# A forgetting-attention and gated-FFN kernel: weight loads tied to the vector engine's progress, and a shallower load queue in its scheduler

## The chip, the cores and the metric

The kernel runs on one core of a Trainium2 chip. The core has a matrix engine (TensorE, PE in the profile), a vector engine (VectorE, DVE), an engine for activation functions (ScalarE, ACT), a general-purpose engine (GpSimd, POOL) and a sync engine (SyncE, SP). Each runs its own instruction stream in program order and waits on semaphores for the others. Loads and stores are issued by SP, ACT or POOL and carried out by 16 DMA engines that all of them share. On-chip tiles live in SBUF; PE writes its results into PSUM.

The metric is the device time of the core in microseconds (us), the median of several runs. The profile is of one execution, and its times count from the start of that execution.

## The reference

Eight batches, each with 8 heads, 576 positions and head size 64, go through causal attention with a decay per position, and then through a gated feed-forward layer with a convolution over positions.

```python
# attention: q, k, v are (8, 8, 576, 64), f is (8, 8, 576)
scores = scale * np.matmul(q, k.transpose(0, 1, 3, 2))
cum    = np.cumsum(np.log(np.clip(f, 0.0001, 1.0)), axis=-1)
scores = np.where(causal, -1e9, scores + cum[..., :, None] - cum[..., None, :])
attn   = softmax(scores)                    # written out in the reference
x      = (attn @ v) as (8, 576, 512)
# feed-forward: w_in (512, 1024), conv_w (3, 1024), w_out (1024, 512)
h    = np.maximum(x @ w_in, 0.0)
conv = sum(conv_w[k] * shifted(h, k) for k in range(3))
out  = (h * sigmoid(conv)) @ w_out
```

## The kernel before

The work is cut into half batches of four heads (called `hb`, 16 of them). Each half batch needs its q and k, loaded with a transpose, its v, and a few extra rows of decay sums in the q and k tiles. Four tiles each for q and k (`RING = 4`) let loads run ahead. A pair of heads inside a half batch is numbered `i`.

SP issues the loads of q, k and v. POOL issues the decay rows and the two weight matrices, which are converted from float32 to float16 on their way:

```python
def rows_of(hb):                      # decay rows of a half batch, issued by POOL
    nc.gpsimd.dma_start(tq[0:1, 0:HS], kd[...])
    nc.gpsimd.dma_start(<two rows of tk>, kd[...])

def load_w_out(j):                    # one of four pieces, 256 KB each on chip
    nc.gpsimd.dma_start(w_out_f16[:, 2 * j:2 * j + 2, :], moe_w_out[256 * j:256 * (j + 1), :]...)
```

DVE prepares what has landed. `clamp` rewrites the q or the k tile of a half batch in place, `cast_v` converts v to float16 in three instructions, and `norm` divides an attention output by its row sums:

```python
def clamp(hb, side, h0, nh): nc.vector.tensor_scalar(t, t, lim..., op0=ALU.mult, op1=ALU.add)
def cast_v(hb, p, eng):      eng.tensor_scalar(va[...], vf[...], 1.0, 0.0, ...)
def norm(i):                 nc.vector.reciprocal(rc, O[...]); nc.vector.tensor_tensor(xn, O, rc, ...)
```

PE computes scores, applies them to v (`pv`, into the single PSUM buffer `O`), transposes the normalized result for some batches (`xpose_pe`; the others are transposed by DMA, issued by SP, in `xpose`), and runs the two matrix products of the feed-forward layer, `moe1` with `w_in_f16` and `moe2` with `w_out_f16`.

The order of the instructions is not written by hand. The Python code describes each piece of work as a task with the engine and the time that it is thought to take, the tasks that it comes after, and a key (low keys go first):

```python
def task(engines, after, key, fn, take=None, give=None, lag=0.2, dma=0.0, also=None, behind=None): ...

    if hb in (2, 3):                                  # in the loop over half batches
        for x, j in zip(landed, (2 * hb - 4, 2 * hb - 3)):   # landed: the loads of q and k
            t_wout.append(task({"POOL": 0.8}, [x], 2 * hb - 1.0, lambda j=j: load_w_out(j), lag=2.0, dma=1.7))
    ...
    for p in range(2):
        t_cast[hb, p] = task({"DVE": 0.75 if p == 0 else 0.42}, [t_half or t_v[b]] + ..., 
                             lambda hb=hb, p=p: cast_v(hb, p, nc.vector), lag=0.2)
        if hb == 1 and p:
            t_win = task({"POOL": 1.0}, [t_cast[1, 1]], -0.5, lambda: nc.gpsimd.dma_start(w_in_f16, ...),
                         lag=2.0, dma=6.5)
```

A small list scheduler, `play()`, goes through these tasks when the kernel is built and writes down, engine by engine, the order in which they are emitted. It holds a load on SP back while more than `QUEUED` microseconds of transfers stand ahead of it by its own count:

```python
AHEAD, QUEUED = 10.0, 6.0
...
if dma and e == "SP" and dma_free > clock + QUEUED:
    kept.append((key, k))
    heapq.heappush(heap, (dma_free - QUEUED, -1, None))
    continue
```

What `play()` settles is an order only. On the chip an instruction waits for what its data need: that a tile was written before it is read, and that it is no longer in use before it is overwritten. A task that comes after another in the list, but shares no data with it, waits for nothing on the chip. The loads of the weights are such tasks: nothing has written or read `w_in_f16` or `w_out_f16` before them.

Of the kernel before, what the change touches and what calls it, by code (L numbers as in the profile page):

```python
# [18 lines left out]
def kernel(  # L19
# [11 lines left out]
    nc = tc.nc  # L31
# [37 lines left out]
    w_in_f16 = cpool.tile([128, NCC, D_FF], FP16)  # L69
    w_out_f16 = cpool.tile([128, NFF, D_MODEL], FP16)  # L70
# [62 lines left out]
    def rows_of(hb):  # L133

        tq, tk = stq_t[hb % RING], stk_t[hb % RING]
        c = slice(hb * HH, (hb + 1) * HH)
        nc.gpsimd.dma_start(tq[0:1, 0:HS], kd[0:1, c, :].rearrange("j h s -> j (h s)"))
        row = HS + 64
        nc.gpsimd.dma_start(bass.AP(tensor=tk.tensor, offset=int(tk.offset) + 2 * row,  # L139
                                    ap=[[2 * row, 2], [1, HS]]),  # L140
                            kd[:, c, :].rearrange("j h s -> j (h s)"))

    def load_w_out(j):

        nc.gpsimd.dma_start(w_out_f16[:, 2 * j:2 * j + 2, :],
                            moe_w_out[256 * j:256 * (j + 1), :].rearrange("(ffc p) dm -> p ffc dm", p=128))
# [10 lines left out]
    def cast_v(hb, p, eng):  # L157
        vf, va = vf_t[hb // 2 % 2][:, HH * (hb % 2):HH * (hb % 2 + 1)], va_t[hb % 3]
        if p == 0:
            eng.tensor_scalar(va[:, 0:2, 0:4, 0:64], vf[:, 0:2, 0:4, :], 1.0, 0.0, op0=ALU.mult, op1=ALU.add)  # L160
            eng.tensor_scalar(va[0:SL, :, 4, 0:64], vf[0:SL, :, 4, :], 1.0, 0.0, op0=ALU.mult, op1=ALU.add)
        else:
            eng.tensor_scalar(va[:, 2:4, 0:4, 0:64], vf[:, 2:4, 0:4, :], 1.0, 0.0, op0=ALU.mult, op1=ALU.add)
# [141 lines left out]
    def off_scores(i, s):  # L305
        hb, h = where(i, s)
        sc = sc_of[i, s] = sc_pool.tile([128, 1024], FP32, name="sc")
        for m in (0, 3, 1, 2):
            w = S - 128 * (m + 1)
            scores(sc[:, OFF[m]:OFF[m] + w], hb, h * S + 128 * m, h * S + 128 * (m + 1), w)  # L310
# [5 lines left out]
    def diag_scores(i):  # L316
        sc = sc_of[i, 2] = sc_pool.tile([128, 1024], FP32, name="sc")
        for s in range(2):
            hb, h = where(i, s)
            nc.tensor.matmul(sc[:, 512 * s:512 * (s + 1)], identb, trib, start=True, stop=False,  # L320
                             skip_group_check=True)
            for m in range(4):
                o, c = h * S + 128 * m, 512 * s + 128 * m
                scores(sc[:, c:c + 128], hb, o, o, 128, False, m == 3)
# [57 lines left out]
    def xpose_pe(b, tb):  # L382

        g, j = grp_of[b]
        if tb == 0 and j == 0:
            xt_of[g] = xt_pool.tile([128, NCC, GROUPS[g][1] * S], FP16, name="xt",
                                    padded_shape=[128, NCC, 2 * S])
        n = 128 if tb < NKB - 1 else SL
        ps = mm_of["x", b, tb] = mm_pool.tile([128, 512], FP32, name="mm")
        p16 = ps.bitcast(FP16)  # L390
        for cc in range(NCC):
            nc.tensor.transpose(p16[:, 128 * cc:128 * cc + n],
                                xn_of[b][0:n, tb, 128 * cc:128 * (cc + 1)], ident16[0:n, 0:n])
# [11 lines left out]
    def tiles_of(g):  # L405
        nb = GROUPS[g][1]
        nt = 3 if nb == 2 else 2
        return nt, nb * S // nt

    def moe1(g, ff, t):  # L410
        nt, w = tiles_of(g)
        xt = xt_of[g]
        ps = mm_of[g, ff, t] = mm_pool.tile([128, 512], FP32, name="mm")
        for cc in range(NCC):
            nc.tensor.matmul(ps[:, 0:w], w_in_f16[:, cc, 128 * ff:128 * (ff + 1)],  # L415
                             xt[:, cc, w * t:w * (t + 1)], start=(cc == 0), stop=(cc == NCC - 1))
# [21 lines left out]
    def conv(g, ff, part):  # L438
        nb, ht = GROUPS[g][1], ht_of[g, ff]
        hl, hc, hr = (ht[:, 0:nb, HT_0 + o:HT_0 + o + S] for o in (-1, 0, 1))  # L440
        if part == 0:
            u_of[g, ff] = u_pool.tile([128, nb, S], FP32, name="u", padded_shape=[128, 2, S])
        u = u_of[g, ff]
        if part == 0:
            nc.vector.scalar_tensor_tensor(u, hl, cwt[:, ff, 0:1], hc, op0=ALU.mult, op1=ALU.add)  # L445
        else:
            nc.vector.scalar_tensor_tensor(u, hr, cwt[:, ff, 1:2], u, op0=ALU.mult, op1=ALU.add)  # L447
# [71 lines left out]
    def task(engines, after, key, fn, take=None, give=None, lag=0.2, dma=0.0, also=None, behind=None):  # L519

        tasks.append((engines, key, fn, [r for r in (take, also) if r], give or [], lag, dma))
        after = [a for a in after if a is not None]
        left.append(len(after) + (behind is not None))
        due.append([])
        next_of.append([])
        if behind is not None:
            next_of[behind].append(len(tasks) - 1)
        for a in after:
            due[a].append(len(tasks) - 1)
        return len(tasks) - 1  # L530
# [10 lines left out]
    t_gate, t_cast, t_xt0, t_wout = {}, {}, {}, []  # L541
# [5 lines left out]
    for hb in range(NHB):  # L547
# [3 lines left out]
        even, landed = [], []  # L551
        for s in range(2):
            if hb == 1:
                x = task({"ACT": 0.01}, [], -9, lambda: None, lag=(0.3, 3.8)[s])
# [17 lines left out]
            last = t_v[b] = task({"SP": 3.5}, [t_cast[2 * b - j, p] for j in (4, 3) for p in range(2)] if b >= 2 else [],  # L572
                                 key + 1.2, lambda b=b: load_v(b), lag=2.3, dma=6.0, behind=last)
        if hb in (2, 3):
            for x, j in zip(landed, (2 * hb - 4, 2 * hb - 3)):
                t_wout.append(task({"POOL": 0.8}, [x], 2 * hb - 1.0, lambda j=j: load_w_out(j), lag=2.0, dma=1.7))
        if hb:
            t_rows[hb] = even + [task({"POOL": 1.1}, [landed[0], even[1]], 2 * hb - 3.0 if hb > 1 else -1.0,
# [3 lines left out]
        for p in range(2):  # L582
            t_cast[hb, p] = task({"DVE": 0.75 if p == 0 else 0.42},
                                 [t_half or t_v[b]] + ([t_pv[2 * hb - 5, 1]] if hb >= 3 else []), 2 * hb - 2.1 + 0.5 * p,
                                 lambda hb=hb, p=p: cast_v(hb, p, nc.vector), lag=0.2)
            if hb == 1 and p:
                t_win = task({"POOL": 1.0}, [t_cast[1, 1]], -0.5, lambda: nc.gpsimd.dma_start(
                    w_in_f16, moe_w_in.rearrange("(cc p) ff -> p cc ff", p=128)), lag=2.0, dma=6.5)

        for p in range(2):  # L590
# [3 lines left out]
            if p == 0:  # L594
                x = t_second = task({"ACT": 0.01}, [], -9, lambda: None, lag=3.7) if i == 0 else None
# [5 lines left out]
            x = task({"PE": 0.9}, t_rows[hb], i + 0.1, lambda i=i: diag_scores(i), take="sc")  # L601
            t_qk[hb, p] = [t_tail, x]
            mask = task({"ACT": 1.02}, [x], i + 0.1, lambda i=i: diag_exp(i), take="pm", give=[("sc", x)])
            for s in range(2):
                x = task({"PE": 0.46}, t_rows[hb], i + 0.2 + 0.4 * s, lambda i=i, s=s: off_scores(i, s),
                         take="sc")
# [10 lines left out]
        if hb % 2:  # L617
            norms = [t_norm[i - j] for j in range(PPB)]
            if b in (0, 1, 2, B - 1):
                t_xt[b] = []  # L620
                for tb in range(NKB):
                    x = task({"PE": 0.27}, norms, i + 0.3 + 0.1 * tb, lambda b=b, tb=tb: xpose_pe(b, tb),
                             take="mm", also="xt" if tb == 0 and grp_of[b][1] == 0 else None, behind=x if tb else None)
# [14 lines left out]
    for g, (b0, nb) in enumerate(GROUPS):  # L638
        nt, w = tiles_of(g)
        n = nb * S  # L640
        t_m1, t_tanh = [], []
        for ff in range(NFF):
            key = start[g] + (start[g + 1] - start[g]) * ff / NFF
            relus = []
            for t in range(nt):
                x = task({"PE": 4 * w / 2400.0}, [x for j in range(nb) for x in t_xt[b0 + j]] + [t_win],
                         key + 0.05 * t,
                         lambda g=g, ff=ff, t=t: moe1(g, ff, t), take="mm", also="ht" if t == 0 else None,
                         behind=t_m1[-1] if t else None)
# [5 lines left out]
            x = task({"DVE": 0.23 + n / 1020.0}, [y], key + 0.14, lambda g=g, ff=ff: conv(g, ff, 1))  # L655
            x = task({"ACT": 0.19 + n / 1200.0 + (1.3 if (g, ff) == (LAST, 0) else 0.0)},
                     [x] + (t_tanh[0:1] or t_exp), key - 0.5, lambda g=g, ff=ff: tanh(g, ff),
                     give=[("u", y)], take="hg" if ff == 0 and g % 2 == 0 else None)
# [9 lines left out]
        x = None  # L668
        if g == LAST:
            banks = [task({"PE": 0.01}, t_xt[b0], start[g] + 0.01 * j, lambda p=p, r=r: last_bank(p, r), take=r)  # L670
                     for j, (p, r) in enumerate(((sc_pool, "sc"), (sc_pool, "sc"), (o_pool, "O")))]
            for ff in range(NFF):
                x = task({"PE": 1.1}, [t_gate[g, ff]] + t_wout + banks + [x] * (ff > 0), start[g], lambda ff=ff: moe2_last(ff))
        for c in chunks:
            key = start[g + 1] + (start[g + 2] - start[g + 1]) * (c - chunks[0]) / len(chunks) + 1.0
            if g == LAST:
                x = t_m2[0] if t_m2 else x
            else:
                x = task({"PE": 1.73}, done + t_wout, key, lambda g=g, c=c: moe2(g, c), take="mm")
            t_m2.append(x)  # L680
            x = task({"DVE": 0.62, "ACT": 0.57}, [x] + ([y] if c % 2 else []), key - 1.0,
                     lambda e, g=g, c=c: evac(g, c, e), give=[("mm", x)] if g < LAST else [], take="ob" if c % 2 == 0 else None)
# [4 lines left out]
        if g % 2:  # L687
            task({"SP": 0.01}, t_m2, key, lambda: None, give=[("hg", t_hg)])

    AHEAD, QUEUED = 10.0, 6.0  # L690

    def play():
        busy = {"PE": 11.5, "ACT": 12.0, "DVE": 12.0, "POOL": 14.0, "SP": 19.0}
# [112 lines left out]
```

## Time and profile before

| what | value |
|---|---|
| time, median of 3 runs | 296.53 us (295.26 to 297.28) |
| span of the profiled execution | 293.7 us |
| PE busy | 248.1 us, 84% of the span |
| DVE busy | 220.5 us, 75% |
| ACT busy | 208.3 us, 71% |
| POOL busy | 35.1 us, 12% |
| transfers | 46.64 MB, mean 159 GB/s |

Busy time is a mean over the whole span. The stages differ: by the table of stretches PE was busy for 18.84 of the 20 us from 160 to 180, but for 5.69 of the 10 us from 20 to 30. So a stretch has to be looked at by itself. The chain of work that ended last gives the waits that set the end; an idle time anywhere else costs nothing. In the lines of a timeline, the first two numbers are the start and the duration in microseconds, L and a number is the line of the kernel, and the bracket at the end holds the idle time before the instruction and what ended it. The granted clock (PEclk) is the share of PE's full clock that it was given.

### The profile page before, as it was taken

To read this page: it belongs to the slowest core of one execution; us is meant where nothing else is said; L and a number is where in the kernel's file an instruction comes from. 1 tells how busy PE (TensorE), PEld (TensorE's weight loads), DVE (VectorE), ACT (ScalarE), POOL (GpSimd) and SP (SyncE) were. 2 spreads that over 40 slices of the span, in tenths; PEclk is the share of its full clock that TensorE was granted. 3 is DMA by queue.
4 is the path that set the end of the run, shared out by engine and by line. 5 is a ranking of instruction groups with operands and counts; after the bars stand their busy time and mean duration, and the time that the engine had idled before them with its cause. 6 is when DMAs were issued, how large, how long until landed. Compare 5 with 4: busy or idle time off the path is not lost.

```text
span 293.7 us, 6359 instructions
## 1 busy us (share of the span) xinstructions
PE 248.1 (84%) x2522; PEld 166.8 (57%) x2522; DVE 220.5 (75%) x389; ACT 208.3 (71%) x345; POOL 35.1 (12%) x85
## 2 busy tenths in 40 slices
PE   3784579858899989999799989993999999769980
PEld 1353457635666766766576766662777765434530
DVE  5942335987789989898778999956788887785661
ACT  4265237749678998797887796984689996774651
POOL 4570020202022022022010001210000000000000
PEclk9979558969799999999999999998899999999996
DMA  7999999999999998899799799997114201020114
GB/s 147 226 174 186 217 175 202 200 218 224 210 190 201 231 211 200 151 228 142 174 244 214 104 278 201 238 201 171 59 42 104 83 2 71 0 110 0 71 74 179
DMA packets 131459, 46.64 MB, mean 159 GB/s; under 512 B 124401, under 2 KB 125425, under 8 KB 131430
## 3 DMA queue, kind: packets, MB, share of 16 engines
q1 hardware_dynamic: 127408, 40.13, 69.8%
q0 software_dynamic: 3696, 5.95, 9.9%
q8 instruction: 20, 0.33, 0.5%
q10 hardware_dynamic: 326, 0.17, 0.3%
q14 instruction: 9, 0.07, 0.1%
HBM read 14.01 MB, written 9.58 MB: 80 GB/s over the span
## 4 chain that ended last, share of the span: by engine, by line
PE 55%; issue 12%; DMA 10%; ACT 10%; SPq 7%; DVE 2%; POOL 1%; ACTq 0%; POOLq 0%
PE mm L477 18%; PE mm L415 15%; PE sc L288 9%; PE O L346 6%; DMA stq<-in_q_dram 5%; SPq L110 4%; PE sc L320 4%; ACT hg L457 3%; ACT po L314 2%; SPq L378 2%; DMA stk<-in_k_dram 2%; ACT ht L428 2%; PE sc L490 2%; DMA stk<-kd 2%; SPq L153 1%
## 5 line engine op out<-in xcount | busy, mean ns | idle before, releaser
L415 PE MATMUL mm<-xt,w_in_f 128*128 128x288 f16 x512 | 80.9, 292 | 4.8 <-DMA xt<-xn 1.8
L288 PE MATMUL sc<-stq,stk 128*128 128x128 bf16 (+3 forms) x576 | 70.4, 252 | 8.4 <-DMA stk<-kd 5.0
L314 ACT ACTIVATE po<-sc 128x1024 f16<-128x1024 f32 x64 | 65.5, 1032 | 7.6 <-PE sc L288 7.1
L445 DVE SCALAR_TENSOR_TENSOR u<-ht,cwt 128x576 f32<-128x576 f16 x64 | 51.5, 812 | 18.6 <-ACT ht L428 15.6
L288 PEld LDWEIGHTS <-stk 128*128 128x128 bf16 x576 | 44.7, 103 | 36.0 <-issue 13.4
L428 ACT ACTIVATE ht<-mm 128x288 f16<-128x288 f32 x128 | 51.7, 416 | 16.7 <-PE mm L415 14.5
L415 PEld LDWEIGHTS <-w_in_f 128*128 128x128 f16 x512 | 47.8, 99 | 22.3 <-issue 7.1
L477 PE MATMUL mm<-w_out_f,hg 128*128 128x512 f16 x248 | 58.6, 379 | 2.1 <-ACT ht L428 2.0
L447 DVE SCALAR_TENSOR_TENSOR u<-ht,cwt,u 128x576 f32<-128x576 f16 x64 | 51.3, 811 | 0.6
L465 DVE SCALAR_TENSOR_TENSOR hg<-hg,ht 128x576 f16<-128x576 f16 x56 | 41.9, 752 | 8.9 <-ACT hg L457 8.5
L457 ACT ACTIVATE hg<-u,cwt 128x576 f16<-128x576 f32 x56 | 43.3, 778 | 4.8 <-DVE u L447 4.7
L328 ACT ACTIVATE pm<-sc 128x1024 f16<-128x1024 f32 x32 | 33.0, 1031 | 18.7 <-PE sc L288 18.7
L346 PE MATMUL O<-va,pm 128*128 128x65 f16 x256 | 32.6, 197 | 9.3 <-DVE xn L359 9.3
L346 PE MATMUL O<-va,po 128*128 128x65 f16 x640 | 38.1, 197 | 1.0 <-ACT po L314 0.9
L477 PEld LDWEIGHTS <-hg 128*128 128x128 f16 x248 | 23.8, 98 | 26.0 <-issue 2.7
L346 PEld LDWEIGHTS <-po 128*128 128x128 f16 x640 | 31.8, 100 | 5.6 <-issue 2.1
L346 PEld LDWEIGHTS <-pm 128*128 128x128 f16 x256 | 25.0, 101 | 10.2 <-DVE xn L359 4.3
L320 PE MATMUL sc<-trib,identb 128*128 128x512 bf16 x64 | 26.2, 410 | 1.9 <-ACT po L314 1.9
L359 DVE TENSOR_TENSOR xn<-O,rc 128x640 f16<-128x640 f32 x32 | 26.4, 824 | 1.1
L501 ACT ACTIVATE ob<-mm 128x512 f32<-128x512 f32 x22 | 13.2, 599 | 13.8 <-PE mm L477 13.6
L139 POOL DMA_DIRECT2D stk<-kd x15 | 7.6, 510 | 97.7 <-DVE stk L118 93.5
L118 DVE TENSOR_SCALAR stk<-stk,lim 128x2304 uint16<-128x2304 uint16 (+1 forms) x17 | 14.3, 840 | 4.9 <-DMA stk<-in_k_dram 4.9
(101 smaller groups left out, 179.0 us busy)
## 6 DMA issues: line engine op xcount, KB each, us to landing
out_dram<-ob SPq DMA_DIRECT2D x16, 512.0 KB, 3.4
vf<-in_v_dram SPq DMA_DIRECT2D x24, 256.0 KB, 5.9
stq<-zq_src POOLq DMA_DIRECT2D x12, 283.5 KB, 5.1
vf<-in_v_dram SPq DMA_DIRECT2D x22, 128.0 KB, 3.6
w_in_f<-in_moe_w_in_dram POOLq DMA_DIRECT2D x1, 1024.0 KB, 10.4
w_out_f<-in_moe_w_out_dram POOLq DMA_DIRECT2D x4, 256.0 KB, 8.6
out_dram<-ob SPq DMA_DIRECT2D x4, 256.0 KB, 3.3
xt<-xn SPq DMA_TRANSPOSE x20, 2.6
```

What stands on the lines that cost most here:

```text
L288: nc.tensor.matmul(sc, stk_t[hb % RING][:, k0:k0 + 128], stq_t[hb % RING][:, q0:q0 + w], start=start, stop=stop, skip_group_check=True)
L314: nc.scalar.activation(p_of[i, s][:, 0:1024], sc_of.pop((i, s)), AF.Exp, scale=SCALE)
L320: nc.tensor.matmul(sc[:, 512 * s:512 * (s + 1)], identb, trib, start=True, stop=False, skip_group_check=True)
L328: nc.scalar.activation(p_of[i, 2], sc_of.pop((i, 2)), AF.Exp, scale=SCALE)
L346: nc.tensor.matmul(O[:, s, 65 * Q:65 * (Q + 1)], w, va[:, h, m, :], start=(m == 0), stop=(m == Q))
L415: nc.tensor.matmul(ps[:, 0:w], w_in_f16[:, cc, 128 * ff:128 * (ff + 1)], xt[:, cc, w * t:w * (t + 1)], start=(cc == 0), stop=(cc == NCC - 1))
L428: nc.scalar.activation(ht[:, 0, HT_0 + w * t:HT_0 + w * (t + 1)], ps[:, 0:w], AF.Relu)
L445: nc.vector.scalar_tensor_tensor(u, hl, cwt[:, ff, 0:1], hc, op0=ALU.mult, op1=ALU.add)
L447: nc.vector.scalar_tensor_tensor(u, hr, cwt[:, ff, 1:2], u, op0=ALU.mult, op1=ALU.add)
L457: nc.scalar.activation(hv, u, AF.Tanh, scale=cwt[:, ff, 2:3])
L465: nc.vector.scalar_tensor_tensor(hv, hv, 1.0, hc, op0=ALU.add, op1=ALU.mult)
L477: nc.tensor.matmul(ps, chunk(g, ff, c), w_out_f16[:, ff, :], start=(ff == 0), stop=(ff == NFF - 1))
```

## The change

Before each load of a weight piece, DVE writes one element of the tile that the load will fill. The load must then wait for this write, since it overwrites the same element. The write itself comes, in DVE's program order, after the conversion or the clamp that the task list had named as the load's predecessor: after the last conversion of the v values of half batch 1 for `w_in`, and after the clamp of q and the clamp of k of half batches 2 and 3 for the four pieces of `w_out`. So the loads of weights are held back on the chip as well, and not in the builder's plan alone. The purpose is to keep their transfers from standing beside the first loads of q, k and v.

The second part sets `QUEUED` from 6.0 to 4.0. The loads of q, k and v are chained to one another in the list, so their own order cannot change by it. What can change is where stores and the transposes by DMA stand between them in SP's stream.

```diff
--- before.py
+++ after.py
@@ -139,6 +139,10 @@
         nc.gpsimd.dma_start(bass.AP(tensor=tk.tensor, offset=int(tk.offset) + 2 * row,
                                     ap=[[2 * row, 2], [1, HS]]),
                             kd[:, c, :].rearrange("j h s -> j (h s)"))
+
+    def hold(w):
+
+        nc.vector.memset(w[0:1, 0, 0:1], 0.0)
 
     def load_w_out(j):
 
@@ -572,7 +576,8 @@
             last = t_v[b] = task({"SP": 3.5}, [t_cast[2 * b - j, p] for j in (4, 3) for p in range(2)] if b >= 2 else [],
                                  key + 1.2, lambda b=b: load_v(b), lag=2.3, dma=6.0, behind=last)
         if hb in (2, 3):
-            for x, j in zip(landed, (2 * hb - 4, 2 * hb - 3)):
+            for x, j in zip(even, (2 * hb - 4, 2 * hb - 3)):
+                x = task({"DVE": 0.1}, [x], -9, lambda j=j: hold(w_out_f16[:, 2 * j:2 * j + 2, :]))
                 t_wout.append(task({"POOL": 0.8}, [x], 2 * hb - 1.0, lambda j=j: load_w_out(j), lag=2.0, dma=1.7))
         if hb:
             t_rows[hb] = even + [task({"POOL": 1.1}, [landed[0], even[1]], 2 * hb - 3.0 if hb > 1 else -1.0,
@@ -584,7 +589,8 @@
                                  [t_half or t_v[b]] + ([t_pv[2 * hb - 5, 1]] if hb >= 3 else []), 2 * hb - 2.1 + 0.5 * p,
                                  lambda hb=hb, p=p: cast_v(hb, p, nc.vector), lag=0.2)
             if hb == 1 and p:
-                t_win = task({"POOL": 1.0}, [t_cast[1, 1]], -0.5, lambda: nc.gpsimd.dma_start(
+                x = task({"DVE": 0.1}, [t_cast[1, 1]], -9, lambda: hold(w_in_f16))
+                t_win = task({"POOL": 1.0}, [x], -0.5, lambda: nc.gpsimd.dma_start(
                     w_in_f16, moe_w_in.rearrange("(cc p) ff -> p cc ff", p=128)), lag=2.0, dma=6.5)
 
         for p in range(2):
@@ -687,7 +693,7 @@
         if g % 2:
             task({"SP": 0.01}, t_m2, key, lambda: None, give=[("hg", t_hg)])
 
-    AHEAD, QUEUED = 10.0, 6.0
+    AHEAD, QUEUED = 10.0, 4.0
 
     def play():
         busy = {"PE": 11.5, "ACT": 12.0, "DVE": 12.0, "POOL": 14.0, "SP": 19.0}
```

## The prediction

> **What bounds the kernel now.** I read the page's forty slices first, to find where PE is not kept busy, then a table of stretches over the start, then the timelines of POOL, SP, DVE and PE there, and last the chain of work that ended last and the list of waits.
>
> ```profile
> PE   3784579858899989999799989993999999769980
> ...
> PEclk9979558969799999999999999998899999999996
> DMA  7999999999999998899799799997114201020114
> ```
>
> A slice is 293.7 / 40 = 7.3 us. From slice 11 (81 us) to slice 27 PE is at nine tenths or close to it: there the kernel is bound by PE. In the first ten slices PE has 3 to 8 tenths, its clock falls to half, and the DMA engines are full. Time lost there is lost for good, since PE has little room later to catch up. The stretches of the start (busy us of each engine with its number of instructions, granted clock, DMA share, GB/s):
>
> ```profile
> 24.00:29.00 5.00, 1.11 (x13) 0.73 (x13) 1.57 (x4) 2.11 (x3) 0.00 (x0) 1.00 1.18 181
> 29.00:34.00 5.00, 3.70 (x46) 2.85 (x45) 0.25 (x1) 2.05 (x2) 0.00 (x0) 0.58 1.27 208
> 34.00:38.00 4.00, 2.15 (x33) 1.89 (x33) 3.76 (x14) 0.00 (x0) 0.52 (x1) 0.50 0.99 220
> 38.00:41.30 3.30, 2.04 (x18) 1.62 (x18) 1.56 (x3) 1.17 (x2) 1.99 (x3) 0.50 1.24 119
> ```
>
> From 24 to 41.3 us PE was busy for 1.11 + 3.70 + 2.15 + 2.04 = 9.0 of 17.3 us, much of it at a clock of about 0.5. No compute engine is full in all four rows, but the DMA share is about 1 in each. What was in flight? The timeline of POOL:
>
> ```profile
> 17.43 0.53 POOL L137 DMA_DIRECT2D stq<-kd  x1
> 17.95 0.53 POOL L139 DMA_DIRECT2D stk<-kd  x1
> 18.47 0.87 POOL L587 DMA_DIRECT2D w_in_f<-in_moe_w_in_dram  x1
> 19.33 1.44 POOL L145 DMA_DIRECT2D w_out_f<-in_moe_w_out_dram  x2
> 34.92 0.52 POOL L137 DMA_DIRECT2D stq<-kd  x1 [14.15 <-DVE rc L357]
> ```
>
> POOL reached the weights at 18.47 us and issued w_in and two pieces of w_out with no idle time before them. The plan meant w_in to follow the conversions of v of half batch 1, which end at 27.8. It is this that the change repairs. What the weights met, on SP and then on DVE:
>
> ```profile
> 19.49 9.73 SPq L110 DMA_TRANSPOSE stq<-in_q_dram  x1
> 29.26 4.44 SPq L110 DMA_TRANSPOSE stk<-in_k_dram  x1
> ```
>
> ```profile
> 27.17 0.29 DVE L161 TENSOR_SCALAR va<-vf 64x256 f16<-64x256 f32 x1 [4.87 <-DMA vf<-in_v_dram]
> ...
> 33.75 0.88 DVE L118 TENSOR_SCALAR stq<-stq,lim 128x2304 uint16<-128x2304 uint16 x1 [4.97 <-DMA stq<-in_q_dram]
> ```
>
> The issue of q of half batch 2 held SP for 9.73 us, where the median issue of a q load is 3.40 us. DVE stood 4.87 us for v and 4.97 us for that q. DVE works in order, so the normalizations behind these two waits came late too, and PE with them: it sat idle 3.67 us before 28.92 and 2.97 us before 35.67, both times until DVE had freed the O buffer. The chain of work confirms it: its longest early piece is this one.
>
> ```profile
> 19.49 14.23 DMA stq<-in_q_dram
> 33.75 0.88 DVE stq L118
> ```
>
> **What the Trainium skill says.** "DMA: Bandwidth & Descriptors", section "Issuing engines are not separate DMA queues", says that transfers issued from different engines run on the same 16 DMA engines and interleave. The trace agrees: q took 14.23 us from issue to landing beside the weights, against a median of 7.1 us for the q loads. The same page, "Queues, rings and completion order", says that a DMA engine takes a ring's descriptors in order and goes round the queues packet by packet. So a delayed w_in would stand ahead of later small transfers of POOL, and would still share with SP's. No line of the trace before shows the first by itself. "TensorE: Matmul & The Clock Gate", section "What's actually happening", says that an idle PE falls to half its clock and gets the full one after some 3.4 us of work. The table above agrees: 0.58 and 0.50 after the idle 24 to 29.
>
> **Part 1: the holds.** They add five writes of one element. A write of this size took 0.059 us before (L240), so 0.3 us of DVE in all; nothing. What they move:
>
> (a) *w_in goes later.* The conversions of v of half batch 1 need v landed. Its last pieces were issued until 19.44. The median landing of v pieces of this size (128 KB) is 3.6 us, so about 23; DVE's three conversions take 0.43 + 0.29 + 0.41, about 1.1 us. The first of these had run at 21.87 before. They end near 23.5, not 27.8: 4 us gained. Then hold, semaphore and issue, and w_in is in flight from about 24.5. At its old 10.4 us it lands near 35.
>
> (b) *q of half batch 2 comes sooner.* Issued at 19.5 with only v ahead, at the median 7.1 us it lands near 26.6, not 33.7: 7 us. k follows, now with w_in beside it. With the q issue at its 3.4 us median, the k issue starts near 23 and, given a slowed issue and landing of 6.6 us as before plus some, is in by about 31. It was clamped at 36.85: some 6 us gained.
>
> (c) *DVE and PE.* Normalization of pair 1 moves from 27.7 to about 23.5, of pair 2 from 34.5 to about 28, of pair 3 from 37.6 to about 32. The transposes and the first product with w_in start 3.6 us after the last (41.29 - 37.64), so near 35.5, just as w_in lands. The decay rows of half batch 2 go out after the clamp of k; they landed at 43.0 - 38.0 = 5.0 us after issue, so its scores begin near 37 instead of 43. I take 5.5 us for the shift, the mean of 6 and what is at risk if w_in lands a little late.
>
> (d) *Does the shift last to 80 us?* From 47.5 to 65 DVE is nearly without idle time and sets the pace (9.62 of the 10 us from 48 to 58). The clamps of half batch 3, at 54.21 and 56.40, show no wait for a transfer; nor does that of k of half batch 4, at 67.85. Their data have room. Two pieces of w_out (38.5 us) also move behind the clamps of half batch 3, off the loads of q and k of it. w_out is first used at 85.2. So most of the shift stays: I subtract 1 us for the bytes, which have to be moved all the same. Against this stands the clock: from 29 to 48 PE was busy 3.70 + 2.15 + 2.04 + 6.35 = 14.2 us at a clock of 0.50 to 0.59. With fewer holes part of it, I guess a fifth of the surplus of 7 us over full clock, is saved: 1 us. Sum of part 1: -5.5 + 1 - 1 = -5.5 us.
>
> (e) *And to the end?* SP waits for PE or for DVE to free q and k tiles for some 47 us (the waits on line 110: 15.1 + 11.1 + 5.8 + 4.3 + 3.8 + 3.6 + 3.3), so loads later have slack and PE sets the pace. I take the 5.5 us through.
>
> **Part 2: QUEUED 4.** Loads keep their order, and the first store stands at 94.30, the first transpose by DMA at 134.83, so the start cannot change by it. Later it may put a transpose ahead of one load. The one place where the chain leaves PE after 80 us is this:
>
> ```profile
> 192.76 3.46 SPq L110
> 196.31 1.22 SPq L378
> ...
> 202.22 2.35 DMA xt<-xn
> 204.61 1.12 PE mm L415 x4
> ```
>
> There PE had 1.28 of 4.6 us from 200 to 204.6. If the transpose goes ahead of the last k load, up to 3.46 us come back; but the scores of the last half batch then wait for that load, and the gain may be eaten. I give it 0, with 2 us either way.
>
> Sum: 296.5 - 5.5 + 0 = 291.0 us.
>
> **The rivals.** *The bytes are the bound:* with a DMA share of 1.0 to 1.2 from 10 to 80 us, delaying a transfer only reorders, and half batch 3 starts where it did. Against it: its clamps did not wait for data. If it holds, only the two pieces of w_out that leave (3.4 us by the kernel's own count) are gained, and the clock's 1 us lost again: 293 to 295. *w_in becomes the new wait:* if q and k slow it beyond 10.4 us, the first product waits, and POOL's in-order stream and ring hold the rows of half batch 2 behind it. 2 to 4 us of the gain go: 293 to 295. *The new SP order stalls loads behind stores:* then PE waits for q or k between 100 and 200 us, where it now has little idle time; +2 to +6 us: 293 to 297. *The gain is larger:* the clock stays at full speed from 29 us on, saving up to 5 of the 7 us, and the transposes come sooner: 286 to 288.
>
> **Range and chances.** The first three rivals pull up to 295 or so, the last down to 287; a single one of them at full size seems as much as one in ten would exceed. So 286.8 to 295.3. Faster by over 2% means below 290.6, just under my middle: 0.45. Slower by over 2% (above 302.5) would need the whole gain undone and 6 us more: 0.05. The rest, 0.50.
>
> **What would show it.** Right: POOL idle before w_in until DVE near 23.5; the q clamp of half batch 2 near 27 with a wait under 2 us; q's issue near 3.5 us; PE's two waits on xn under 2 us each; first product with w_in near 36; clock above 0.6 from 29 to 48. Wrong: the product waits for w_in; the scores of half batch 3 (62.36 before, after a wait of 3.47 us for stk) start less than 3 us sooner; PE shows new waits for q, k or xt after 100 us.

## The result, and the profile after

The changed kernel takes 285.71 us (median of 4 runs, 285.54 to 286.53). The kernel before, run beside it, takes 295.89 us. The ratio is 0.9701, with a 95% interval of 0.9608 to 0.9794: 3.0% faster, or 8.9 us of 296.5. Some executions run slower as a whole; ratios here and below leave them out, so 0.9701 is not the quotient of the two medians, and no stage times are taken from the profiles of experiments 2, 4 and 12, which fell on such executions. The prediction, 291.0 us, was a ratio of 0.981. The direction was right and the size too small, 5.5 us against 8.9. The measured median lies 1.1 us under the stated range of 286.8 to 295.3; the ratio, applied to the 296.5 us that the prediction started from, gives 287.7 us, just inside it.

The forty slices of the changed kernel, as they were read for the kernel before (a slice is now 284.7 / 40 = 7.1 us):

```profile
PE   3959479588999999998999899975999999789980
...
PEclk9999659979999999999999999997899999999997
DMA  8999999999999999997999999999213301110114
```

PE is full from slice 10 (71 us) on, one slice and 10 us sooner. The stretches of the start, with the same limits as before:

```profile
24.00:29.00 5.00, 4.53 (x89) 3.72 (x88) 3.49 (x11) 4.05 (x5) 0.79 (x1) 1.00 1.17 214
29.00:34.00 5.00, 1.10 (x13) 0.77 (x10) 2.41 (x9) 0.59 (x1) 2.51 (x4) 0.73 1.16 221
34.00:38.00 4.00, 1.85 (x18) 1.30 (x17) 0.51 (x2) 0.96 (x2) 0.00 (x0) 0.50 1.37 214
38.00:41.30 3.30, 3.30 (x21) 2.13 (x19) 0.00 (x0) 1.41 (x2) 0.00 (x0) 0.50 1.07 186
```

The stretch from 24 to 29 us, nearly empty before (1.11 us of PE), is now full (4.53 us). The hole now comes later, from 29 to 38 us, and is shorter. The DMA share is as high as it was. POOL, SP and DVE of the changed kernel:

```profile
18.05 0.53 POOL L139 DMA_DIRECT2D stk<-kd  x1
23.99 0.80 POOL L593 DMA_DIRECT2D w_in_f<-in_moe_w_in_dram  x1 [5.41 <-DVE rc L361]
29.54 0.71 POOL L149 DMA_DIRECT2D w_out_f<-in_moe_w_out_dram  x1 [4.76 <-DVE w_out_f L145]
```

```profile
20.15 2.77 SPq L110 DMA_TRANSPOSE stq<-in_q_dram  x1
22.97 3.01 SPq L110 DMA_TRANSPOSE stk<-in_k_dram  x1
```

```profile
23.62 0.06 DVE L145 MEMSET w_in_f<- 1x1 f16 x1
...
26.04 0.88 DVE L118 TENSOR_SCALAR stq<-stq,lim 128x2304 uint16<-128x2304 uint16 x1 [1.30 <-DMA stq<-in_q_dram]
...
30.99 0.88 DVE L118 TENSOR_SCALAR stk<-stk,lim 128x2304 uint16<-128x2304 uint16 x1 [1.74 <-DMA stk<-in_k_dram]
```

POOL now stands 5.41 us until DVE has written the one element, and w_in goes out at 23.99 instead of 18.47. (The line names the next instruction of DVE, a reciprocal that touches nothing of w_in; in experiment 11 the same wait is put down to the write itself, L145.) The issue of q takes 2.77 us instead of 9.73, and the clamp of q starts at 26.04 instead of 33.75. PE's remaining waits at the start are these:

```profile
32.91 0.71 PE L396 MATMUL mm<-ident,xn 128*128 128x128 f16 x5 [3.65 <-DVE w_out_f L145]
37.73 0.40 PE L292 MATMUL sc<-stq,stk 128*128 128x64 bf16 x4 [1.91 <-DMA stk<-kd]
57.43 0.28 PE L292 MATMUL sc<-stq,stk 128*128 128x64 bf16 x4 [3.56 <-DMA stk<-kd]
```

The first line has to be read with care. The releaser named is the one-element write for w_out, but PE reads xn there. The last normalization ends at 32.85, and the write at 32.86 is only the next event of DVE. The real cause is that normalization, which stood behind the clamp of k at 30.99. The two others are waits for the decay rows of half batches 2 and 3. They end 5.3 and 4.9 us sooner than for the same scores before:

```profile
42.99 0.39 PE L288 MATMUL sc<-stq,stk 128*128 128x64 bf16 x4 [0.35 <-DMA stk<-kd]
62.36 0.37 PE L288 MATMUL sc<-stq,stk 128*128 128x64 bf16 x4 [3.47 <-DMA stk<-kd]
```

So the start went as the theory of the holds has it. But does holding the transfers explain 8.9 us? The change also adds five tasks to the list and alters QUEUED, and each of these makes the scheduler write another order. Compared engine by engine, POOL and SP of the kernel before and of the holds with QUEUED 6 agree but for one piece of w_out; on PE, DVE and ACT the orders part from half batch 2 on. The experiments separate the three parts.

### The profile page after: what moved, and what is told of

Read it like the earlier page. It is cut to its first block, busy times and chain, and to the rows that moved or that the text cites. A ratio compares the mean times of both kernels' runs of the same rounds, so it can differ in the third digit from the quotient of the medians.

```text
span 284.7 us, 6362 instructions
## 1 busy us (share of the span) xinstructions
PE 243.1 (85%) x2522; PEld 163.4 (57%) x2522; DVE 219.9 (77%) x393; ACT 208.9 (73%) x346; POOL 35.1 (12%) x85
## 4 chain that ended last, share of the span: by engine, by line
PE 47%; DMA 16%; ACT 11%; SPq 10%; DVE 8%; issue 4%; POOL 0%; ACTq 0%; DVEq 0%; POOLq 0%
PE mm L481 14%; PE mm L419 13%; PE sc L292 9%; PE O L350 5%; DMA stk<-in_k_dram 5%; SPq L110 5%; ACT po L318 4%; DMA stk<-kd 4%; PE sc L324 3%; SPq L382 3%; ACT hg L461 3%; DMA vf<-in_v_dram 2%; DMA stq<-kd 2%; SPq L157 2%; DVE hg L469 2%
## 5 line engine op out<-in xcount | busy, mean ns | idle before, releaser
L292 PE MATMUL sc<-stq,stk 128*128 128x128 bf16 (+3 forms) x576 | 67.6, 246 | 10.2 <-DMA stk<-kd 6.7
L432 ACT ACTIVATE ht<-mm 128x288 f16<-128x288 f32 x128 | 51.0, 414 | 20.6 <-PE mm L419 18.5
L292 PEld LDWEIGHTS <-stk 128*128 128x128 bf16 x576 | 43.0, 100 | 34.1 <-issue 10.4
L350 PE MATMUL O<-va,po 128*128 128x65 f16 x640 | 37.0, 194 | 1.2 <-ACT po L318 1.2
L350 PEld LDWEIGHTS <-po 128*128 128x128 f16 x640 | 30.8, 98 | 4.1 <-ACT po L318 1.9
L350 PE MATMUL O<-va,pm 128*128 128x65 f16 x256 | 31.4, 195 | 1.3 <-DVE xn L363 1.3
L350 PEld LDWEIGHTS <-pm 128*128 128x128 f16 x256 | 24.5, 99 | 3.4 <-DVE xn L363 1.4
L324 PE MATMUL sc<-trib,identb 128*128 128x512 bf16 x64 | 25.4, 398 | 1.0 <-ACT po L318 0.7
## 6 DMA issues: line engine op xcount, KB each, us to landing
w_in_f<-in_moe_w_in_dram POOLq DMA_DIRECT2D x1, 1024.0 KB, 10.5
```

The source lines that it names most:

```text
L292: nc.tensor.matmul(sc, stk_t[hb % RING][:, k0:k0 + 128], stq_t[hb % RING][:, q0:q0 + w], start=start, stop=stop, skip_group_check=True)
L350: nc.tensor.matmul(O[:, s, 65 * Q:65 * (Q + 1)], w, va[:, h, m, :], start=(m == 0), stop=(m == Q))
L432: nc.scalar.activation(ht[:, 0, HT_0 + w * t:HT_0 + w * (t + 1)], ps[:, 0:w], AF.Relu)
```

## Experiments

Ratios are against the kernel before, with 95% intervals.

**1 to 4: held or not, in two orders.** To keep an order and drop the hold, the write goes to an element that nothing else uses:

```diff
 def hold(w):
-    nc.vector.memset(w[0:1, 0, 0:1], 0.0)
+    nc.vector.memset(spare, 0.0)        # spare: a tile of one element
```

Experiment 1 has this edit and QUEUED 6. Experiment 2 is the change with QUEUED 6 (`- QUEUED = 4.0`, `+ QUEUED = 6.0`). Experiment 3 is the change with this edit. Experiment 4 is the change itself.

Experiment 1, the order of the holds with QUEUED 6, nothing held:

> The same list of tasks as with the holds and QUEUED 6, so the same order on every engine as a kernel with the holds alone, but the five writes go to a spare element: no load of weights waits. Theory (the transfers that are kept apart are the cause of the early gain): the start looks as before, with w_in issued near 18.5 us and the first product with w_in near 41, and the time is that of before within 1 us (ratio 0.997 to 1.003). Rival (the five extra tasks shift the order and this is what helps): the time falls by 3 us or more although nothing is held.

Experiment 2, the holds alone:

> The holds as in the change, QUEUED left at 6. Theory (the holds give some 5.5 us, as the prediction had it, and the rest of the 9 us comes from the order that QUEUED 4 makes): ratio about 0.982, the scores of half batch 2 near 37.5 us. Rival (the holds give all of it, and the further gain after 75 us follows from an earlier start): ratio about 0.970.

Experiment 3, the order of the changed kernel, nothing held:

> Exactly the order of the changed kernel on every engine, but the five writes go to a spare element, so no load of weights waits. Theory (holds 5.5 us, order 3.5 us, and they add): ratio about 0.988, and the first product with w_in near 41 us as before. Rival (the order does nothing by itself): ratio 1.00. Second rival (the order does all): ratio 0.97.

Experiment 4, the changed kernel again:

> The changed kernel beside the other three on the same chip, to complete the table of two orders by held or not: ratio 0.97 again, between 0.961 and 0.979.

| | nothing held | held |
|---|---|---|
| order with QUEUED 6 | 0.9951 (0.9906 to 0.9996) | 0.9871 (0.9759 to 0.9982) |
| order with QUEUED 4 | 0.9769 (0.9701 to 0.9836) | 0.9698 (0.9635 to 0.9760) |

Read down, QUEUED 4 takes off 1.8% without the holds and 1.7% with them: some 5.2 us. Read across, the holds take off 0.8% and 0.7%: some 2.2 us, each difference within the uncertainty of its two ratios, but the same twice. The five tasks' effect on the order, from 1 to 0.9951, is about 1.5 us by the ratio, whose interval only just leaves 1 out; the medians of all 22 executions of experiment 1 and of all 27 of the kernel before beside it are 296.09 and 296.15 us, so this part is not shown. The three add up to the 8.9 us, as steps between the same kernels must. The theory that I took into these runs (5.5 us from the holds, 3.5 from the order) has its two parts the wrong way round. The rival that all comes from the holds fails by experiment 2, and the one that the order does nothing by experiment 3. That the order does all (0.97) lies at the edge of experiment 3's interval; what speaks against it is the first column of the next table.

**Where the two parts lie.** The table takes, from each profile, the start of the first scores of half batch 5, then the time to the masks of the last half batch's tail scores, then the rest:

| profile | order | held | to half batch 5 | to the tail of half batch 15 | rest | span |
|---|---|---|---|---|---|---|
| before | before | no | 89.4 | 143.2 | 61.1 | 293.7 |
| experiment 1 | QUEUED 6 | no | 85.2 | 145.1 | 61.3 | 291.6 |
| experiment 9 (below) | QUEUED 6 | yes | 82.9 | 145.0 | 61.3 | 289.2 |
| experiment 3 | QUEUED 4 | no | 84.6 | 143.7 | 60.1 | 288.4 |
| changed | QUEUED 4 | yes | 82.0 | 142.6 | 60.1 | 284.7 |
| experiment 10 (below) | QUEUED 4 | yes | 82.6 | 143.9 | 60.1 | 286.6 |

The holds shorten the first column alone: 84.6 to a mean of 82.3, and 85.2 to 82.9, 2.3 us both times. QUEUED 4 shortens the two others: 1.2 us of the rest, always the same, and 1 to 2 us of the middle. The order that the five tasks make works on the start as well: with nothing held, half batch 5 begins 4.2 us sooner (89.4 to 85.2), and the middle loses 1.9 us of that again. So of the 7.4 us by which the changed kernel reaches half batch 5 sooner than the kernel before, 4.8 are there in experiment 3, without any hold, and 2.6 come with the holds. Each row is a single profile. Experiment 3's POOL shows that its first column is of a kernel without holds:

```profile
18.81 0.95 POOL L595 DMA_DIRECT2D w_in_f<-in_moe_w_in_dram  x1
```

The rest, from the tail scores of half batch 15, in the table of stretches for the kernel before and then for the changed one:

```profile
232.60:293.70 61.10, 48.43 (x366) 28.40 (x363) 40.65 (x61) 38.49 (x71) 0.00 (x0) 0.96 0.17 65
```

```profile
224.60:284.70 60.10, 49.00 (x384) 29.24 (x382) 41.78 (x63) 38.29 (x71) 0.00 (x0) 0.96 0.18 68
```

The changed kernel has more PE work left here (384 matmuls against 366, 49.00 us against 48.43) and still ends it 1.0 us sooner; the transfers are no part of it (a DMA share of 0.17 and 0.18). One wait of PE stands for most of that. In the kernel before:

```profile
264.29 1.89 PE L477 MATMUL mm<-w_out_f,hg 128*128 128x512 f16 x8 [1.74 <-ACT ht L428]
```

It is there in experiments 1 and 9 too (1.74 us at 262.04 and 259.62), and not in the changed kernel, nor in 3 or 10, whose longest wait for ACT there is this:

```profile
249.39 1.14 PE L419 MATMUL mm<-xt,w_in_f 128*128 128x288 f16 x8 [0.77 <-ACT ht L432]
```

**5 to 8: is it the depth of the queue, or the order that the number makes?** All have the holds. Experiments 5 and 6 switch QUEUED within the plan, 7 and 8 set it to 3.5 and 8:

```diff
-AHEAD, QUEUED = 10.0, 4.0
+AHEAD, QUEUED, LATER, SWITCH = 10.0, 4.0, 6.0, 90.0     # experiment 6: 6.0, 4.0
 ...
-if dma and e == "SP" and dma_free > clock + QUEUED:
+queued = QUEUED if clock < SWITCH else LATER
+if dma and e == "SP" and dma_free > clock + queued:
```

Experiment 5, QUEUED 4 and then 6:

> The holds, QUEUED 4 in the list scheduler up to its own time of 90 us and 6 after it. The scheduler's own count of the end is 277.4 us for this order, against 277.9 for the changed kernel, 283.7 for the holds with QUEUED 6. Theory (QUEUED works only by the order that it happens to make, and the chip follows the scheduler's count): about 287 us, ratio 0.970. Rival (fewer transfers in flight help the late stage, between 90 and 200 us, by themselves): nearer to the holds alone, ratio 0.98 to 0.987.

Experiment 6, QUEUED 6 and then 4:

> The holds, QUEUED 6 up to the scheduler's time of 90 us and 4 after it. The scheduler counts 280.5 us. Theory (the order counts, as planned): between the two, about 290 us, ratio 0.979. Rival (a shallower queue in the late stage is what helps): as the changed kernel, ratio 0.970. Second rival (a shallower queue in the start is what helps): as the holds alone, ratio 0.987.

Experiment 7, QUEUED 3.5:

> The holds, QUEUED 3.5. The scheduler counts 277.8 us, as for 4. Both the theory of the order and that of the depth say about 287 us, ratio 0.970; a ratio of 0.98 or more would say that the result of QUEUED 4 is a stroke of luck that neither explains.

Experiment 8, QUEUED 8:

> The holds, QUEUED 8. The scheduler counts 282.9 us, 0.8 less than for 6. Theory of the order: about 293.5 us, ratio 0.984. Rival (the depth by itself costs time, 6.5 us from 4 to 6): slower than the holds with 6, 297 us or more, ratio 1.00 or more.

| experiment | QUEUED | ratio (95% interval) | the scheduler's count of the end, us |
|---|---|---|---|
| 5 | 4, then 6 | 0.9686 (0.9617 to 0.9754) | 277.4 |
| changed (4) | 4 | 0.9698 (0.9635 to 0.9760) | 277.9 |
| 7 | 3.5 | 0.9704 (0.9604 to 0.9804) | 277.8 |
| 6 | 6, then 4 | 0.9745 (0.9678 to 0.9812) | 280.5 |
| 8 | 8 | 0.9765 (0.9681 to 0.9850) | 282.9 |
| 2 | 6 | 0.9871 (0.9759 to 0.9982) | 283.7 |

The rival of the depth falls with experiment 8: a deeper queue than 6 is no slower, but by its middle value 1% faster. A shallow queue in the first half alone gives as much as one throughout (experiment 5), so it is not the depth in the late stage; in the second half alone (experiment 6) it falls between its theory (0.979) and its rival (0.970), and the interval holds both. By the middle values the chip puts the six in nearly the same rank as the scheduler's count, but most of the intervals overlap. The sizes do not follow: experiment 8 was expected at 0.984 from its count. So QUEUED works by the order that it makes, and the order of 6 has the poorest middle value among those tried.

**9 and 10: one exchange in SP's stream.** With QUEUED 6, q of half batch 11 is issued ahead of the transposes of batch 3; with 4, behind them. Both experiments move that one load after the plan is made, and leave every other engine as it was:

```diff
 order, est = play()
+move(t_load[11, 0], t_xt0[3], 1)     # behind the transposes; experiment 10: 0, ahead of them
```

Experiment 9, the holds with QUEUED 6 and the load put back:

> The holds with QUEUED 6, and one change in SP's stream alone: the load of q of half batch 11 goes behind the transposes of batch 3 instead of ahead of them, as it does with QUEUED 4. All other engines keep the order of QUEUED 6. Theory A (this one exchange on SP, which brings x of batch 3 to PE 5 us sooner, is what QUEUED 4 brings): nearly the changed kernel, 288 to 289 us, ratio 0.973 to 0.977. Theory B (what counts is that the orders of PE, DVE and ACT were planned anew around it): as the holds with QUEUED 6, ratio 0.984 to 0.988.

Experiment 10, the changed kernel and the load put ahead:

> The changed kernel with the same exchange undone on SP alone: q of half batch 11 ahead of the transposes of batch 3. Theory A: most of the gain of QUEUED 4 goes, ratio 0.980 to 0.987. Theory B: no change beyond 1 us, ratio 0.968 to 0.974, since the orders of PE, DVE and ACT stay.

Experiment 9 gave 0.9894 (0.9828 to 0.9959), like the 0.9871 without the exchange. Experiment 10 gave 0.9735 (0.9669 to 0.9800), like the 0.9698 without it. SP did issue the transposes at 126.10 us in experiment 9, and at 129.51 instead of 124.71 in experiment 10, so the exchange took place; the time did not follow. Theory A falls.

SP's two streams differ in more than that. With QUEUED 4 the transposes of batch 5 also go ahead of the last k load, which is the exchange that the prediction had named. In the changed kernel, and then in experiment 9, SP and PE have these lines there:

```profile
187.64 7.00 SPq L382 DMA_TRANSPOSE xt<-xn  x5
...
195.38 3.01 SPq L110 DMA_TRANSPOSE stk<-in_k_dram  x1
...
194.03 0.65 PE L419 MATMUL mm<-xt,w_in_f 128*128 128x288 f16 x4 [3.96 <-DMA xt<-xn]
195.90 1.12 PE L419 MATMUL mm<-xt,w_in_f 128*128 128x288 f16 x4 [1.22 <-DMA xt<-xn]
```

```profile
188.11 3.15 SPq L110 DMA_TRANSPOSE stk<-in_k_dram  x1
191.35 7.41 SPq L382 DMA_TRANSPOSE xt<-xn  x5
...
196.26 0.22 PE L350 MATMUL O<-va,pm 128*128 128x65 f16 x1 [3.61 <-DVE xn L363]
199.90 1.12 PE L419 MATMUL mm<-xt,w_in_f 128*128 128x288 f16 x4 [1.26 <-DMA xt<-xn]
```

PE stands 5.2 us with the transposes ahead and 4.9 us with them behind, so the profiles show no gain from it; no run has it alone. What is left for the gain of QUEUED 4 is the rest of the order, on PE, DVE and ACT, with which POOL's shifts as well, and the stores in SP's stream. Which of these it is was not separated.

**11 and 12: which hold, and what is left at half batch 3.** Experiment 11 sends the four writes for w_out to the spare element and keeps that for w_in:

```diff
-x = task({"DVE": 0.1}, [x], -9, lambda j=j: hold(w_out_f16[:, 2 * j:2 * j + 2, :]))
+x = task({"DVE": 0.1}, [x], -9, lambda j=j: free_of_it(...))      # writes spare
```

> The order of the changed kernel on every engine; w_in is held by its write, the four writes for w_out go to a spare element. Theory (w_in stood first and longest beside the loads, so its hold gives the gain of the holds): ratio 0.970 as with all holds. Rival (the pieces of w_out matter as well): halfway to the unheld kernel in that order, ratio 0.973 or more.

It gave 0.9773 (0.9704 to 0.9843), against 0.9698 with all holds (and about 0.9735 for the two other forms of the changed kernel measured beside it, experiments 10 and 12); its profile was the shortest of all (282.3 us, half batch 5 at 81.8 us). The ratio speaks for the rival and the profile for the theory, and the intervals overlap. Which hold it is stays open.

Experiment 12 moves the loads of w_out back in POOL's stream, by the same means as in 9:

```diff
+for j, r in ((0, 3), (1, 3), (2, 4), (3, 4)):
+    move(t_wout[j], t_rows[r][-1], 1)
```

> The changed kernel with the four loads of w_out moved back in POOL's stream alone, two behind the decay rows of half batch 3 and two behind those of half batch 4. Theory (the shift won by the holds shrinks at half batch 3 since the rows stand behind pieces of w_out and share the engines with them): PE's wait for the rows of half batch 3 falls from 3.56 to under 2 us, its first scores come near 56 instead of 57.4 us, ratio about 0.965. Rival (the bytes of q, k and v set it): the wait stays above 3 us, ratio 0.970.

It gave 0.9736 (0.9655 to 0.9818), no gain, which gives no support to the theory that the rows of half batch 3 wait behind pieces of w_out in POOL's stream. It does not test whether they share the DMA engines with them: POOL issued two pieces right behind these rows, at 53.77 us after 53.27.

## Why the prediction was right in direction and wrong in its parts

*(a) and (b), the transfers: right.* w_in was expected to go out from about 24.5 and to land near 35; it was issued at 23.99 and took 10.5 us, as long as before (10.4). The clamp of k was expected at about 31 and came at 30.99. q took 5.9 us from issue to landing instead of 14.2. k, now beside w_in, took 8.0 instead of 6.6, which agrees with what "DMA: Bandwidth & Descriptors" in the Trainium skill says under "Issuing engines are not separate DMA queues", that transfers of different issuers interleave on the same DMA engines. That w_in alone makes the 1.4 us is not shown.

*(c) PE at half batch 2: right for the normalizations and the scores, wrong for the first product.* Normalization of the three pairs was expected near 23.5, 28 and 32 and came at 23.66, 26.83 and 31.78. PE's two waits for it before 28.92 and 35.67 (3.67 and 2.97 us) are down to 0.6 us or less, as expected, but the one before the transposes grew from 0.94 to the 3.65 us shown above. The scores were expected near 37 and began at 37.73. The product with w_in was expected near 35.5 and came at 40.48. w_in had landed by then. The five tasks had moved this product behind the scores of half batch 2 in PE's stream, where the kernel before has it ahead of them (41.29 against 42.99). I had worked on the order of before.

*(d) "So most of the shift stays": this step failed.* In the order of QUEUED 4, unheld and held, the first scores start at:

| half batch | experiment 3, unheld | changed, held | shift |
|---|---|---|---|
| 2 | 42.15 | 37.73 | -4.4 |
| 3 | 60.51 | 57.43 | -3.1 |
| 4 | 70.21 | 67.62 | -2.6 |
| 5 | 84.62 | 82.03 | -2.6 |

The shift that the holds make begins at 4.4 us and not at 5.5, and of these 1.8 are lost by half batch 5; I had subtracted 1 for the bytes and given it back for the clock. The clock's part is not what was wrong: up to half batch 5 PE was busy for 61.45 us in experiment 3 and for 60.08 in the changed kernel, with 676 matmuls recorded in both. Part of the loss is a wait that grew. The decay rows of half batch 3 were issued at 56.42 us in experiment 3 and at 52.49 in the changed kernel, but took 4.1 us to reach PE there and 4.9 here. PE's wait for them went from 2.71 us to the 3.56 shown above:

```profile
60.51 0.28 PE L294 MATMUL sc<-stq,stk 128*128 128x64 bf16 x4 [2.71 <-DMA stk<-kd]
```

So the term of -5.5 us for part 1 measured -2.2, and with the 1.5 us of the new tasks' order, which I had not counted and which is not shown, -3.7. The first rival, that the bytes are the bound, comes nearer in size (3.4 us gained, less 1 for the clock), but not in mechanism: half batch 3 started 3.1 us sooner, where the rival had it start no sooner. What slows these rows is not settled; experiment 12 found no gain in moving pieces of w_out behind them. Step (e), that what is left at half batch 5 lasts to the end, agrees: 2.6 us there and some 2.2 in the time.

*Part 2, "I give it 0, with 2 us either way": this step failed too*, and by more. It measured -5.2 us. I took QUEUED to act on SP's stream alone, and looked for a transpose that might pass a load. The one that I named, ahead of the last k load, did pass it, and PE stood there as long as with QUEUED 6 (5.2 and 4.9 us), so the 0 fits that exchange; the wait of 3.96 us for xt is also one of the signs that I had listed for being wrong, and the kernel gained all the same. Experiments 9 and 10 show that another exchange, at batch 3, does not carry the gain either. The number changes when the plan thinks a load has landed, and with that the order on PE, DVE and ACT. "The start cannot change by it" rested on the same mistake, though the result bears it out: 85.2 and 84.6 us to half batch 5.

*The sum* came as near as it did partly by luck, since the errors have opposite signs, and it was too small because they did not cancel: 3.3 us too much for the holds against 5.2 and 1.5 too little for the order. The fourth rival named the size that came (286 to 288 us), but for another reason, a clock at full speed from 29 us on; it was 0.50 from 34 to 41.3. Of the 5.2 us the profiles place 1.2 in the rest after the tail of half batch 15 and 1 to 2 in the middle. The remainder is within what single profiles vary by and is not placed.

## What to carry to other kernels

A load into a buffer that nothing has touched goes out as soon as its in-order issuer gets to it, whatever the plan says (here at 18.47 us, where the plan meant a point after 27.8). If its transfer would stand beside more urgent ones, a one-element write behind the right instruction ties it down for 0.06 us; here that was worth some 2 us. In a kernel whose order a list scheduler writes, an edit of a task or of a parameter can also change the order on all engines; run the same order without the effect as a control before the effect is given the credit, and try neighbouring values of the parameter before its meaning is believed.

## What was not expected of the hardware

Two things. A deeper load queue cost nothing that shows: QUEUED 8 gave 0.9765 and 6 gave 0.9871, though the order differs between the two as well. And filling the hole at the start did not keep PE's clock up through it. In the changed kernel PE had been busy for 4.53 of the 5 us from 24 to 29, but then stood 3.65 us before 32.91. In windows of one microsecond its clock is 1.00 up to 31 us, 0.63 from 31 to 32, 0.50 from 32 to 41 and 1.00 from 42 on. In the kernel before it is 0.50 from 30 to 46 and 1.00 from 47 on, so the shorter hole still cost some ten microseconds at half the clock, against sixteen.
